# Pairing the transfers of K and x, splitting the constants, and moving two gathers, in an attention and mixture-of-experts kernel

## The chip, the core and the metric

The kernel runs on one core of one Trainium2 chip. The metric is the device time of one execution in microseconds (us); lower is better. The engines are called as in the profile: PE is TensorE (PEld its weight loads), DVE is VectorE, ACT is ScalarE, POOL is GpSimd, SP is SyncE, which only issues transfers here. A queue named after an engine (SPq, ACTq, POOLq) is the list of transfers that the engine issues, in program order.

## The reference

Attention within chunks of 64 tokens, for 8 batches of 8 heads with 576 tokens and 64 columns, then a layer of 8 experts on the 4608 rows of 512 columns that attention gives. A row goes to its best expert only where its skip score is positive.

```python
def _attn_ref(q, k, v):
    B, H, S, D = q.shape                       # 8, 8, 576, 64
    ...
    scores = scale * np.matmul(q_c, k_c.transpose(0, 1, 2, 4, 3))
    scores = scores - np.max(scores, axis=-1, keepdims=True)
    attn = np.exp(scores)
    attn = attn / (np.sum(attn, axis=-1, keepdims=True) + 1e-09)
    out = np.matmul(attn, v_c)
    return out.reshape(B, H, S, D).astype(np.float32)

def _moe_ref(x, w_skip, w_gate, w1, w2):
    do_compute = x @ w_skip > 0
    out = x.copy()
    xc = x[do_compute]
    logits = xc @ w_gate
    e_idx = np.argmax(logits, axis=1)
    ...
    for e in range(E):
        mask = e_idx == e
        h = np.maximum(xc[mask] @ w1[e], 0.0)
        y[mask] = gate_w[mask, None] * (h @ w2[e])
    out[do_compute] = xc + y
    return out.astype(np.float32)
```

## The kernel before

**Attention.** The 4608 rows are 36 tiles of 128. For each tile SP loads Q (256 KB), K (two transfers of 128 KB) and V (260 KB). K lands in a block-diagonal tile: the even partitions in half 0, the odd ones in half 1 (`load_qk`, lines 134 to 140), the rest having been set to zero once at the start (lines 149 and 155), so that one matmul against the block-diagonal K gives the scores of two heads. There are six K buffers of one tile each, six Q and six V buffers.

The loop over tiles (line 687) is software-pipelined. In iteration i PE does the scores of tile i (`pe_scores`), the weighted sum with V of tile i-2 (`pe_pv`), the transposes of x of tile i-3 (`pe_xtrans`), the router's logits of tile i-4 (`pe_logits`) and the transposes of the exponentials of tile i-1 (`pe_ptrans`). ACT copies the scores out of PSUM (`ac_scores`), takes the exponentials (`ac_exp`) and copies the two kinds of transposes (`ac_ptrans`, `ac_hi`). DVE takes the maxima (`ve_max`), normalizes into x (`ve_norm`) and makes the low halves of the split numbers (`ve_lo`). POOL subtracts the maxima (`po_sub`). The order of the instructions on each engine is the order of these calls; each engine works through its list in order.

**Transfers.** In iteration i SP issues Q and K of tile i+5 and V of tile i+4. In iterations 2 to 9 it adds one piece of w1 of the first expert (`load_piece`); ACT casts the piece three iterations later and DVE splits it (`conv_w1`). In iterations 10 to 26 it adds the store of one finished tile of x (`store_x`, line 702); the stores pause in iterations 27 to 30 and go on with three tiles each in 31 to 35, where the eight w2 pieces of the first expert follow them, two in each of the iterations 32 to 35. Each transfer is given one of eight completion counters in turn, and its issue waits until the transfer that had this counter before has landed.

**Constants.** All [128, ...] constants lie in one tensor that one transfer brings into `csb`: the identity for the transposes, the router's weights (`wsg`), the counting tables. DVE and POOL turn them into working form in iterations 1 to 7 (`more_constants`).

**Early experts.** Tokens are routed in four groups of 8, 9, 8 and 11 tiles (`route`). As soon as two groups are routed, two blocks of the first expert are known; their rows are gathered back from `out` by POOL (`early_gather`), which is allowed from iteration `GATHER_AT` + m on for block m, and three iterations later PE transposes them (`early_xt`, line 656; the transposes are line 485, ACT's cast 486, DVE's split 487). At most one such event happens in an iteration. After the loop the matmuls of the first expert's first layer (`l1_steps`, line 496) follow.

**Experts.** The other experts' weights (512 KB pieces) are loaded, cast and split while PE works through the blocks, up to the end.

Of the kernel before, what the change touches and what calls it, by code (L numbers as in the profile page):

```python
# [112 lines left out]
def moe_attention_kernel(ctx: ExitStack, tc: tile.TileContext, qk: bass.AP, vv: bass.AP, cst: bass.AP, crow: bass.AP, wall: bass.AP, out: bass.AP):  # L113
    nc = tc.nc
# [17 lines left out]
    kbd = [ap.tile([P, 2, DM], F32, name=f"k{i}", bufs=1) for i in range(KB)]  # L132

    def load_qk(t):
        if t < NT:
            T[t]["q"] = ap.tile([P, DM], F32, name="q", bufs=QB)
            nc.sync.dma_start(T[t]["q"], qk[t, 0])
            T[t]["k"] = kbd[t % KB]
            for a in range(2):
                (nc.scalar if a and t < 2 else nc.sync).dma_start(T[t]["k"].rearrange("(d h) a f -> h d a f", h=2)[a, :, a], qk[t, 1].rearrange("(d h) f -> h d f", h=2)[a])  # L140
# [153 lines left out]
    def ve_norm(t):  # L294
        o, rr = T[t].pop("o")
        nc.vector.reciprocal(rr, rr)
        x = ap.tile([P, DM], F32, name="x", bufs=XB)
# [2 lines left out]
        xq.append((t, x))  # L300

    xq = []

    def store_x(n):
        for _ in range(min(n, len(xq))):
            t, x = xq.pop(0)
            nc.sync.dma_start(out[t * P:(t + 1) * P, :], x)
# [691 lines left out]
```

## Time and profile before

| what | value |
|---|---|
| time, median of 3 runs | 346.68 us (345.04 to 348.3) |
| time of the profiled execution | 345.18 us |
| its span (first to last instruction) | 343.3 us |
| granted TensorE clock, mean | 0.994 |
| PE busy | 322.5 us (94%) |
| DVE busy | 254.3 us (74%) |
| ACT busy | 186.9 us (54%) |
| POOL busy | 110.3 us (32%) |
| moved by DMA | 81.85 MB, 238 GB/s on average |
| loads of Q, K, V, issues | 36, 72, 36 |
| stores of x, issues | 36 |

In the rows of the profile the first number of a timeline row is the start in us and the second the time that the row's instructions took; `[0.55 <-DMA k<-in_qk]` is idle time of the engine before it, and what ended it. In rows of waits stand the total in us, how often, and the longest. In rows of transfers stand their number, the KB of each and the median us from issue to landing. In rows of windows each engine's busy us comes with its number of instructions, then the granted clock, the DMA engines' busy share and the rate.

### The profile page before, as it was taken

What the parts mean: (1) busy time and instruction counts of PE and PEld (TensorE: products, weight loads), DVE (VectorE), ACT (ScalarE), POOL (GpSimd) and SP (SyncE); (2) the same over time, 40 slices, a digit from 0 to 9 for tenths busy, and PEclk for the clock granted to TensorE, in tenths of its full rate; (3) what the DMA queues carried; (4) which work ended last, traced back from release to release, by engine and by line L of the source; (5) the groups of instructions that cost most, each with busy time, mean ns of one, the idle gap of its engine ahead of it and who ended that gap; (6) DMA issues with size and microseconds to landing.
All of it is one profiled execution on the core that took longest, in us unless ns stands there. A gap on an engine that the chain in (4) does not pass through costs nothing.

```text
span 343.3 us, 10130 instructions
## 1 busy us (share of the span) xinstructions
PE 322.5 (94%) x3996; PEld 231.4 (67%) x3996; DVE 254.3 (74%) x489; ACT 186.9 (54%) x361; POOL 110.3 (32%) x110
## 2 busy tenths in 40 slices
PE   7798899999999988999899999999999999999990
PEld 4586788888888877845655456747647659587670
DVE  3668798887988877786769999966867868667230
ACT  1568787787777867403557444554454544456020
POOL 8233323334325405116700347233433322120111
PEclk9999999999999999999999999999999999999997
DMA  7999999999999998009956778767667666562001
GB/s 233 307 323 314 344 347 327 296 309 303 319 331 322 362 324 326 2 11 349 349 190 225 231 257 275 240 201 245 201 187 269 214 216 207 188 213 93 32 25 31
DMA packets 34981, 81.85 MB, mean 238 GB/s; under 512 B 4831, under 2 KB 4832, under 8 KB 34930
## 3 DMA queue, kind: packets, MB, share of 16 engines
q1 hardware_dynamic: 31378, 70.94, 62.6%
q0 software_dynamic: 3104, 9.33, 7.2%
q10 hardware_dynamic: 448, 0.89, 0.7%
q8 instruction: 33, 0.54, 0.6%
q14 instruction: 18, 0.15, 0.1%
HBM read 67.11 MB, written 14.17 MB: 237 GB/s over the span
## 4 chain that ended last, share of the span: by engine, by line
PE 51%; DVE 6%; ACT 2%; issue 1%; POOLq 0%; DVEq 0%; ACTq 0%
PE sp L521 26%; PE hp L496 20%; PE sp L528 3%; PE xt L485 2%; DVE ys L540 2%; DVE ht L501 2%; DVE wset L226 1%; ACT wset L368 1%; ACT ht L500 0%; DVE xt L487 0%; POOLq L995 0%; ACT wst L371 0%; DVE ex L398 0%; ACT wset L225 0%; DVE one L444 0%
## 5 line engine op out<-in xcount | busy, mean ns | idle before, releaser
L496 PEld LDWEIGHTS <-wset 128*128 128x128 f16 x960 | 79.2, 98 | 24.0 <-issue 7.8
L496 PE MATMUL hp<-xt,wset 128*128 128x288 f16 (+8 forms) x900 | 91.4, 262 | 3.5 <-DVE ht L501 3.5
L521 PE MATMUL sp<-wset,ht 128*128 128x512 f16 (+7 forms) x504 | 91.6, 380 | 0.0
L226 DVE SCALAR_TENSOR_TENSOR wset<-wst,wset 128x1024 f16<-128x1024 f32 x56 | 67.6, 1216 | 9.0 <-ACT wset L225 8.9
L521 PEld LDWEIGHTS <-ht 128*128 128x128 f16 (+7 forms) x504 | 40.9, 102 | 40.9 <-issue 1.9
L225 ACT ACTIVATE wset<-wst 128x1024 f16<-128x1024 f32 x56 | 57.9, 1049 | 4.1 <-DMA wst<-in_wall 4.1
L261 POOL TENSOR_TENSOR sc<-sc,mx 128x512 f32<-128x512 f32 x34 | 35.9, 1055 | 70.4 <-DVE mx L252 70.4
L500 ACT ACTIVATE ht<-hp 128x288 f16<-128x288 f32 (+8 forms) x75 | 26.9, 360 | 55.4 <-PE hp L496 54.2
L229 POOL DMA_INDIRECT out<-ys,sidx x18 | 24.9, 1386 | 99.6 <-DVE ys L540 84.8
L501 DVE SCALAR_TENSOR_TENSOR ht<-hp,ht 128x288 f16<-128x288 f32 (+8 forms) x75 | 28.4, 391 | 18.8 <-ACT ht L500 18.1
L242 PE MATMUL spq<-k,q 128*64 128x128 f32 x576 | 40.2, 283 | 0.9 <-DMA k<-in_qk 0.8
L242 PEld LDWEIGHTS spq<-k,q 128*64 128x64 f32 x576 | 31.6, 139 | 7.8 <-issue 6.6
L486 ACT ACTIVATE xt<-xt 128x512 f16<-128x512 f32 (+7 forms) x20 | 10.2, 512 | 43.8 <-PE xt L485 43.8
L252 DVE TENSOR_REDUCE mx<-sc 128x8 f32<-128x512 f32 x34 | 23.2, 683 | 10.6 <-ACT sc L247 9.8
L229 POOL DMA_INDIRECT xg<-out,sidx x18 | 25.5, 1414 | 7.5 <-issue 4.3
L298 DVE TENSOR_TENSOR x<-o,rr 128x512 f32<-128x512 f32 x36 | 24.9, 692 | 3.5
L277 ACT ACTIVATE ps<-pt 128x512 f32<-128x512 f32 x36 | 21.5, 597 | 10.3 <-PE pt L272 9.9
L247 ACT ACTIVATE sc<-spq 128x512 f32<-128x512 f32 x34 | 20.2, 595 | 12.2 <-PE spq L242 12.2
L323 DVE SCALAR_TENSOR_TENSOR xs<-xp,xs 128x512 f16<-128x512 f32 x36 | 24.5, 682 | 1.6 <-ACT xs L318 1.4
L285 PE MATMUL o<-v,ps 64*64 64x65 f32 x1152 | 25.4, 224 | 0.1
L272 PE MATMUL pt<-csb,px 128*128 128x128 f32 x144 | 23.2, 284 | 2.0 <-ACT px L265 1.9
L313 PE MATMUL xp<-csb,x 128*128 128x128 f32 x144 | 23.9, 286 | 1.2 <-issue 0.6
(129 smaller groups left out, 335.2 us busy)
## 6 DMA issues: line engine op xcount, KB each, us to landing
wst<-in_wall SPq DMA_DIRECT2D x56, 512.0 KB, 4.3
q<-in_qk SPq DMA_DIRECT2D x36, 256.0 KB, 5.0
out<-x SPq DMA_DIRECT2D x36, 256.0 KB, 5.1
v<-in_vv SPq DMA_DIRECT2D x35, 260.0 KB, 4.6
k<-in_qk SPq DMA_DIRECT2D x70, 128.0 KB, 4.6
wst<-in_wall SPq DMA_DIRECT2D x16, 256.0 KB, 4.6
csb<-in_cst ACTq DMA_DIRECT2D x1, 348.5 KB, 5.1
xg<-out,sidx POOLq DMA_INDIRECT x18, 6.4
```

The costliest lines, as they stand in the source:

```text
L225: nc.scalar.activation(w[:, 0, fc, :], st, AF.Copy, scale=SW)
L226: nc.vector.scalar_tensor_tensor(w[:, 1, fc, :], st, SW, w[:, 0, fc, :], op0=ALU.mult, op1=ALU.subtract)
L229: ins = nc.gpsimd.indirect_dma_start(**kw)
L242: nc.tensor.matmul(sp[halves[c], 2 * j:2 * j + 2, :], q[:, c, j, :], k[:, c, j], start=True, stop=True, skip_group_check=True)
L261: nc.gpsimd.tensor_tensor(T[t]["sc"], T[t]["sc"], mx, op=ALU.subtract)
L285: nc.tensor.matmul(o[halves[c], a, j * VW:(j + 1) * VW], pt[halves[a], j, halves[c]], v[halves[a], c, j, :], start=True, stop=True, skip_g ...
L298: nc.vector.tensor_tensor(x.rearrange("p (j a d) -> p a j d", j=KC, a=2), o[:, :, :, :D], rr.to_broadcast([P, 2, KC, D]), op=ALU.mult)
L323: nc.vector.scalar_tensor_tensor(xs[:, 1], T[t].pop("xp"), SX, xs[:, 0], op0=ALU.mult, op1=ALU.subtract)
L496: nc.tensor.matmul(hp, w()[:, a, fc, j * P:(j + 1) * P], xt[:, b, j, :n], start=(m == 0), stop=(m == 11))
L500: nc.scalar.activation(ht[:, 0, fc, :n], hp, AF.Relu)
L501: nc.vector.scalar_tensor_tensor(ht[:, 1, fc, :n], hp, 0.0, ht[:, 0, fc, :n], op0=ALU.max, op1=ALU.subtract)
L521: nc.tensor.matmul(y[c * P // cg:c * P // cg + n], ht[:, a, fc, o:o + n], w[:, b, fc, P * KC:], start=(f == 0 and m == 0), stop=(f == fw - ...
```

## The change

K buffers hold two tiles each, three of them. From tile 2 on, K of an even and the following odd tile are loaded together, in two transfers of 256 KB (one for each half of the partitions), in odd iterations and behind the scores of that iteration. The stores of x take two tiles at a time (512 KB): in the even iterations 10 to 26, then two pairs, one, two, one, two in the iterations 31 to 35; the last two tiles are stored singly. The identity has a transfer and a tile of its own (`idt`, 64 KB); the other constants follow V of tile 1 on SP's queue, and the casts of the router's weights and of `iota` move to iterations 3 to 5. At the start Q of tile 2 and half of K of tiles 2 and 3 are issued by ACT. `GATHER_AT` goes from 31 to 30.

```diff
-QB, KB, VB, AHEAD, VAHEAD = 6, 6, 6, 5, 4
+QB, KB, VB, AHEAD, VAHEAD = 6, 3, 6, 5, 4
...
-XB = 16
+XB = 8
...
-GATHER_AT = 31
+GATHER_AT = 30
...
-    kbd = [ap.tile([P, 2, DM], F32, name=f"k{i}", bufs=1) for i in range(KB)]
+    kbd = [ap.tile([P, 2, 2, DM], F32, name=f"k{i}", bufs=1) for i in range(KB)]
...
+    def load_k(t, n=2, eng=(nc.sync, nc.sync)):
+        if t < NT:
+            kp = kbd[t // 2 % KB]
+            u = slice(t % 2, t % 2 + n)
             for a in range(2):
+                eng[a].dma_start(kp.rearrange("(d h) t a f -> h d t a f", h=2)[a, :, u, a], qk[t:t + n, 1].rearrange("t (d h) f -> h d t f", h=2)[a])
+            for i in range(n):
+                T[t + i]["k"] = kp[:, t % 2 + i]
...
-    load_qk(0)
-    load_qk(1)
-    nc.scalar.dma_start(csb, cst)
-    load_v(0)
-    load_qk(2)
-    nc.sync.dma_start(rsb, crow)
-    load_v(1)
-    load_qk(3)
-    load_v(2)
-    load_qk(4)
-    load_v(3)
+    two = nc.sync, nc.scalar
+    for t in range(2):
+        load_q(t)
+        load_k(t, 1, two)
+    nc.scalar.dma_start(idt, cst[:, :P])
+    load_q(2, nc.scalar)
+    load_k(2, 2, two)
+    load_v(0)
+    load_q(3)
+    load_v(1)
+    nc.sync.dma_start(csb, cst[:, P:])
+    load_v(2)
+    load_q(4)
+    load_k(4)
+    load_v(3)
+    nc.sync.dma_start(rsb, crow)
...
-        x = ap.tile([P, DM], F32, name="x", bufs=XB)
+        if t % 2 == 0:
+            xpair[0] = ap.tile([P, 2, DM], F32, name="x", bufs=XB)
+        x = xpair[0][:, t % 2]
...
+        if t >= NT - 2:
+            xq.append((t, 1, x))
+        elif t % 2:
+            xq.append((t - 1, 2, xpair[0]))
...
-            nc.sync.dma_start(out[t * P:(t + 1) * P, :], x)
+            t, m, x = xq.pop(0)
+            o = out[t * P:(t + m) * P, :]
+            nc.sync.dma_start(o if m == 1 else o.rearrange("(t p) f -> p t f", t=m), x)
...
-        load_qk(i + AHEAD)
+        load_q(i + AHEAD)
         on(pe_scores, i)
+        if i % 2:
+            load_k(i + AHEAD)
...
-        store_x(0 if i < X_FROM or X_HOLD <= i < X_REST else 1 if i < X_HOLD else 3)
+        store_x(0 if i < X_FROM or X_HOLD <= i < X_REST else 1 - i % 2 if i < X_HOLD else 1 + i % 2)
```

The order on SP's queue at the start, from the first transfer on; the waits in brackets name the completion counters (DMAHW0 to DMAHW7) and the engines that cleared the K buffers. Before:

```order
L137 DMA q<-in_qk 128x512
L140 DMA k_82<-in_qk 64x512 [waits Pool_49]
L137 DMA q<-in_qk 128x512
L140 DMA k_83<-in_qk 64x512 [waits Pool_49]
L137 DMA q<-in_qk 128x512
L140 DMA k_84<-in_qk 64x512 [waits DMAHW1_49,DVE_49]
L140 DMA k_84<-in_qk 64x512 [waits DMAHW2_49]
L163 DMA rsb<-in_crow 1x360 [waits DMAHW3_49]
L145 DMA v<-in_vv 128x520 [waits DMAHW4_49]
L137 DMA q<-in_qk 128x512 [waits DMAHW5_49]
L140 DMA k_85<-in_qk 64x512 [waits DMAHW6_49,Pool_49]
L140 DMA k_85<-in_qk 64x512 [waits DMAHW7_49]
```

Now:

```order
L137 DMA q<-in_qk 128x512
L144 DMA k_82<-in_qk 64x512 [waits Pool_49]
L137 DMA q<-in_qk 128x512
L144 DMA k_82<-in_qk 64x512 [waits Pool_49]
L144 DMA k_83<-in_qk 64x2x512 [waits DMAHW1_49,DVE_49]
L151 DMA v<-in_vv 128x520 [waits DMAHW2_49]
L137 DMA q<-in_qk 128x512 [waits DMAHW3_49]
L151 DMA v<-in_vv 128x520 [waits DMAHW4_49]
L178 DMA csb<-in_cst 128x569 [waits DMAHW5_49]
L151 DMA v<-in_vv 128x520 [waits DMAHW6_49]
L137 DMA q<-in_qk 128x512 [waits DMAHW7_49]
L144 DMA k_84<-in_qk 64x2x512 [waits DMAHW0_49,Pool_49]
```

K of tile 3 stood in rows 11 and 12 and is now part of row 5; Q of tile 2 has left SP's queue, and V of tiles 0 to 2 and the constants stand between the K of the first four tiles and that of tiles 4 and 5.

The order on SP's queue for two iterations in the middle of attention (iterations with stores), before:

```order
L137 DMA q<-in_qk 128x512
L140 DMA k_82<-in_qk 64x512 x2
L145 DMA v<-in_vv 128x520
L307 DMA out<-x 128x512
L137 DMA q<-in_qk 128x512
L140 DMA k_83<-in_qk 64x512 x2
L145 DMA v<-in_vv 128x520
L307 DMA out<-x 128x512
```

Now:

```order
L137 DMA q<-in_qk 128x512
L144 DMA k_82<-in_qk 64x2x512 x2
L151 DMA v<-in_vv 128x520
L137 DMA q<-in_qk 128x512
L151 DMA v<-in_vv 128x520
L328 DMA out<-x 128x2x512
```

Ten transfers have become seven; K is issued in the odd, x in the even iteration.

The order on PE at the end of the loop, from the transposes of iteration 34 to the first matmul of the first layer (`l1_steps`), without the logits' rows (lines 330 and 351); `rk<-csb,xg` are the transposes of an early block. Before:

```order
L272 MATMUL pt<-csb,px 128x128 x4
L485 MATMUL rk<-csb,xg 128x128 x4
L242 MATMUL spq_156<-k_87,q 64x128 x8
L285 MATMUL o<-v,ps 64x65 x16
L313 MATMUL xp<-csb,x 128x128 x4
...
L272 MATMUL pt<-csb,px 128x128 x4
L485 MATMUL rk<-csb,xg 128x128 x4
L496 LDWEIGHTS wset
L496 MATMUL spq_157<-xt_176,wset 128x256
```

Now:

```order
L287 MATMUL pt<-idt,px 128x128 x4
L506 MATMUL rk<-idt,xg 128x128 x4
L257 MATMUL spq_153<-k_84,q 64x128 x8
L300 MATMUL o<-v,ps 64x65 x16
L334 MATMUL xp<-idt,x 128x128 x4
...
L287 MATMUL pt<-idt,px 128x128 x4
L517 LDWEIGHTS wset
L517 MATMUL spq_154<-xt_173,wset 128x256
```

The second block's transposes no longer stand right ahead of the first layer; they have taken the place of the first block's, which have moved one iteration up.

More of the change, by code (lines that the diff above doesn't have):

```diff
@@ L131, in moe_attention_kernel, with load_q @@
     halves = (slice(0, CH), slice(CH, P))
-    kbd = [ap.tile([P, 2, DM], F32, name=f"k{i}", bufs=1) for i in range(KB)]
-    def load_qk(t):
+    kbd = [ap.tile([P, 2, 2, DM], F32, name=f"k{i}", bufs=1) for i in range(KB)]
+    def load_q(t, eng=nc.sync):
         if t < NT:
             T[t]["q"] = ap.tile([P, DM], F32, name="q", bufs=QB)
-            nc.sync.dma_start(T[t]["q"], qk[t, 0])
-            T[t]["k"] = kbd[t % KB]
+            eng.dma_start(T[t]["q"], qk[t, 0])
+    def load_k(t, n=2, eng=(nc.sync, nc.sync)):
+        if t < NT:
+            kp = kbd[t // 2 % KB]
+            u = slice(t % 2, t % 2 + n)
             for a in range(2):
-                (nc.scalar if a and t < 2 else nc.sync).dma_start(T[t]["k"].rearrange("(d h) a f -> h d a f", h=2)[a, :, a], qk[t, 1].rearrange("(d h) f -> h d f", h=2)[a])
+                eng[a].dma_start(kp.rearrange("(d h) t a f -> h d t a f", h=2)[a, :, u, a], qk[t:t + n, 1].rearrange("t (d h) f -> h d t f", h=2)[a])
+            for i in range(n):
+                T[t + i]["k"] = kp[:, t % 2 + i]
     def load_v(t):
@@ L144, in load_v @@
             T[t]["v"] = ap.tile([P, 2, KC, VW], F32, name="v", bufs=VB)
-            (nc.sync if t else nc.scalar).dma_start(T[t]["v"], vv[t])
+            nc.sync.dma_start(T[t]["v"], vv[t])
     man = tc.manual_schedule()
     man.__enter__()
-    nc.vector.memset(kbd[0][:, 1], 0.0)
+    nc.vector.memset(kbd[0][:, 0, 1], 0.0)
     ones = cpool.tile([P, P], F16, name="ones")
@@ L153, in moe_attention_kernel @@
     nc.vector.memset(zeros, 0.0)
-    for i, k in enumerate(kbd):
-        (nc.vector if i in (2, 4) else nc.gpsimd).memset(k if i else k[:, 0], 0.0)
-    csb = cpool.tile([P, CCOLS], F32, name="csb")
-    rsb = cpool.tile([1, RCOLS], F32, name="rsb")
-    load_qk(0)
-    load_qk(1)
-    nc.scalar.dma_start(csb, cst)
-    load_v(0)
-    load_qk(2)
-    nc.sync.dma_start(rsb, crow)
-    load_v(1)
-    load_qk(3)
-    load_v(2)
-    load_qk(4)
-    load_v(3)
+    nc.gpsimd.memset(kbd[0][:, 0, 0], 0.0)
+    nc.gpsimd.memset(kbd[0][:, 1], 0.0)
+    for m in range(1, KB):
+        for i in range(2):
+            (nc.vector, nc.gpsimd)[m - 1].memset(kbd[m][:, i], 0.0)
+    idt = cpool.tile([P, P], F32, name="idt")
+    csb = cpool.tile([P, CCOLS - P], F32, name="csb")
+    rsb = cpool.tile([1, RCOLS], F32, name="rsb")
+    two = nc.sync, nc.scalar
[5 more added lines that the diff above has]
+    load_k(2, 2, two)
+    load_v(0)
+    load_q(3)
[5 more added lines that the diff above has]
+    load_v(3)
+    nc.sync.dma_start(rsb, crow)
     nc.scalar.activation(cpool.tile([P, 1], F32, name="first"), ones[:, 0:1], AF.Exp)
@@ L180, in C @@
         lo, hi = (_C if name in _C else _R)[name]
-        return (csb if name in _C else rsb)[:, lo:hi]
-    ident = C("ident")
+        return csb[:, lo - P:hi - P] if name in _C else rsb[:, lo:hi]
+    ident = idt
     upper = cpool.tile([P, P], F16, name="upper")
@@ L197, in more_constants @@
     def more_constants(i):
-        if i == DIRECT - 1:
+        if i == 3:
             w = C("wsg").rearrange("p (k n) -> p k n", k=KC)
@@ L201, in more_constants @@
             nc.vector.scalar_tensor_tensor(wsg[:, :, 1], w, SW, wsg[:, :, 0], op0=ALU.mult, op1=ALU.subtract)
-        elif i in (3, 4):
-            r = slice((i - 3) * CH, (i - 2) * CH)
+        elif i in (4, 5):
+            r = slice((i - 4) * CH, (i - 3) * CH)
             nc.vector.tensor_copy(iota[:, r], C("iota")[:, r].unsqueeze(2).to_broadcast([P, CH, G]))
@@ L296, in ve_norm @@
         nc.vector.reciprocal(rr, rr)
[L297 removed]
+        if t % 2 == 0:
+            xpair[0] = ap.tile([P, 2, DM], F32, name="x", bufs=XB)
+        x = xpair[0][:, t % 2]
         nc.vector.tensor_tensor(x.rearrange("p (j a d) -> p a j d", j=KC, a=2), o[:, :, :, :D], rr.to_broadcast([P, 2, KC, D]), op=ALU.mult)
         T[t]["x"] = x
[L300 to L302 removed]
+        if t >= NT - 2:
+            xq.append((t, 1, x))
+        elif t % 2:
+            xq.append((t - 1, 2, xpair[0]))
+    xq, xpair = [], [None]
     def store_x(n):
         for _ in range(min(n, len(xq))):
[L306 to L307 removed]
+            t, m, x = xq.pop(0)
+            o = out[t * P:(t + m) * P, :]
+            nc.sync.dma_start(o if m == 1 else o.rearrange("(t p) f -> p t f", t=m), x)
     def pe_xtrans(t):
```

## The prediction

> **What bounds the kernel now.** I read the chain of waits first, then the windows by stage, then who waited for whom in the first 136 us, then the PE rows in time.
>
> ```profile
> PE 51%; DVE 6%; ACT 2%; issue 1%; POOLq 0%; DVEq 0%; ACTq 0%
> ```
>
> ```profile
> core 0: us, PE busy (x) PEld busy (x) DVE busy (x) ACT busy (x) POOL busy (x), PEclk, DMA share, GB/s
> ...
> 24.00:40.00 16.00, 13.76 (x292) 11.34 (x293) 12.06 (x24) 12.88 (x29) 4.59 (x6) 1.00 0.96 331
> ...
> 56.00:72.00 16.00, 16.00 (x345) 13.89 (x342) 13.41 (x26) 12.49 (x29) 5.34 (x6) 1.00 0.93 291
> ```
>
> The chain is PE's, and PE is busy without a hole in 56 to 72 us at full clock. The change touches only attention and its tail; the expert blocks behind it run the same program, so the end moves by what PE gains or loses in attention. Two things matter there: the holes of PE (2.2 us of 16 in 24 to 40 us), and DMA, which is 93 to 96% busy and so may have no room for a late transfer.
>
> ```profile
> ACT wset L363 <- DMA wst<-in_wall: 2.1, 3, 1.3
> ...
> PE pt L272 <- ACT px L265: 1.9, 3, 1.3
> ```
>
> ```profile
> 10.28 0.65 PE L272 MATMUL pt<-csb,px 128*128 128x128 f32 x4 [1.31 <-ACT px L265]
> 13.72 1.09 PE L242 MATMUL spq<-k,q 128*64 128x128 f32 x16 [0.55 <-DMA k<-in_qk]
> 16.98 1.09 PE L242 MATMUL spq<-k,q 128*64 128x128 f32 x16 [0.24 <-DMA k<-in_qk]
> 26.10 0.20 PE L330 MATMUL lg<-wsg,xs 128*128 128x18 f16 x2 [0.77 <-issue]
> 26.63 0.66 PE L272 MATMUL pt<-csb,px 128*128 128x128 f32 x4 [0.34 <-ACT px L265]
> ```
>
> The reader is to see which holes a transfer opened: 0.55 us at tile 3 and 0.24 us at tile 4 wait for K itself; 0.34 us at 26.63 us waits for an exp that stood behind a weight cast on ACT. The 1.31 us at 10.28 us is the first tile's own max, subtract and exp, and stays. The 0.77 us is "issue": nothing in the trace that this change moves.
>
> **The change part by part.**
>
> *Start: K pair 2/3 ahead of V, identity alone, other constants behind V of tile 1.*
>
> ```profile
> 8.66 1.12 SPq L140 DMA_DIRECT2D k<-in_qk  x2
> ...
> 10.97 1.12 SPq L140 DMA_DIRECT2D k<-in_qk  x2
> ```
>
> From K of tile 3 at 8.66 us to K of tile 4 at 10.97 us SP issues one tile's loads without a pause: 2.31 us for 0.79 MB, so SP itself caps them at about 340 GB/s, and K of tile 3 is the one that came 0.55 us late. After, K of tiles 2 and 3 is issued in the place of K of tile 2, half of it on ACT's queue, and SP issues two transfers for what took it four (1.1 us less a pair). ACT computes nothing before the first exp, which PE has at 10.28 us, so its five issues (the last behind the landing of tile 0's Q) hold nothing up. I remove the 0.55 us. The identity alone lands sooner, but the first transposes wait for the exp anyway: 0. The other constants now go out ahead of V of tile 2; their first use on DVE stands behind the max of tile 3, whose scores start at 13.72 us before, so what hides them is some 4 us of landing time behind an issue near 9 us: 0. Without that cover DVE would stop, in iteration 3, for as long as they are late. The pair 4/5 puts 262 KB more ahead of tile 4's scores: 0.8 us at 331 GB/s, against an SP that is no longer the cap. Bounds for tile 4: its 0.24 us goes, or grows by 0.8; I leave it. **Term 1: -0.55 us (bounds -0.8 to +0.25: both waits go, or tile 3's goes and tile 4's grows by 0.8).**
>
> *Weights of the first expert.* Eight w1 pieces are issued behind the K and V of three later tiles.
>
> ```profile
> 20.41 0.43 SPq L357 DMA_DIRECT2D wst<-in_wall  x1
> ...
> 24.95 0.63 ACT L363 ACTIVATE wset<-wst 128x512 f16<-128x512 f32 x1 [1.30 <-DMA wst<-in_wall]
> ```
>
> The bytes ahead of the first piece are the same before and after (tiles 0 to 7 of Q and K, 0 to 6 of V, the constants: 6.4 MB). It lands at 24.95 us, ACT wanted it 1.30 us before. The stretch from 9 to 25 us need only run 8% faster to cover that. PE's own loss is 1.9 - 1.31 = 0.6 us behind exp; ACT's is 2.1 us. A part of ACT's delay runs on into later tiles, a part hides under the 0.77 us hole: I take 0.8, near the PE row. **Term 2: -0.8 us (bounds -2.1 to 0).**
>
> *K and stores in pairs, from tile 10 on.* Bytes are equal; SP issues 7 transfers for two tiles instead of 10. Each transfer names one of eight completion counters in turn and waits for the one eight before it, so eight are in flight: 8 x 206 KB on average before, 8 x 294 KB after.
>
> ```profile
> DMA packets 9434, 16.90 MB, mean 313 GB/s; under 512 B 1287, under 2 KB 1287, under 8 KB 9422
> ...
> k<-in_qk SPq DMA_DIRECT2D x34, 128.0 KB, 4.6
> ```
>
> ```profile
> DMA packets 4611, 8.78 MB, mean 351 GB/s; under 512 B 545, under 2 KB 545, under 8 KB 4607
> ...
> out<-x SPq DMA_DIRECT2D x19, 256.0 KB, 5.4
> ```
>
> The first fence is 56 to 110 us (mixed sizes), the second 111 to 136 us, where every transfer is 256 KB: with 24% more in flight the rate is 12% higher and the landing 0.8 us longer. That is the nearest row to a queue of pairs, so I take 351 GB/s: 1.053 MB a tile in 3.00 us against 3.36 us at 313. It is needed, since the cover of K shrinks:
>
> ```profile
> 47.15 1.16 SPq L140 DMA_DIRECT2D k<-in_qk  x2
> ...
> 88.53 1.13 SPq L140 DMA_DIRECT2D k<-in_qk  x2
> ```
>
> ```profile
> 57.28 1.09 PE L242 MATMUL spq<-k,q 128*64 128x128 f32 x16
> ...
> 94.42 1.09 PE L242 MATMUL spq<-k,q 128*64 128x128 f32 x16
> ```
>
> These are K of tiles 16 and 28 and their scores. The second half is issued some 0.55 us after the row's start and lands 4.6 us later: 52.3 us for 57.28, a cover of 5.0 us; 93.7 us for 94.42, a cover of 0.7 us. PE takes (94.42 - 57.28) / 12 = 3.10 us a tile and DMA is slower, until stores pause at iteration 27. After, an even tile's K has 262 KB of its neighbour's K and 262 KB of one more stored tile ahead of it: 1.5 us at 351 GB/s. PE being 1.35 us earlier (terms 1 and 2) takes cover too. Against these 2.85 us stands 3.36 - 3.00 = 0.36 us a tile, 4.3 us over the 12 tiles: a cover of 0.7 + 4.3 - 2.85 = 2.2 us is left. **Term 3: 0 (bounds 0 to +1.0, worked out under the rivals).** The Trainium skill, "DMA: Bandwidth & Descriptors", section "Bandwidth", gives 341 GB/s for a transfer of 1 MB; by an estimate from it a tile would take 3.09 us, the gain over 12 tiles would be 3.2 us and the cover 1.1 us instead of 2.2: the sum stays, the wall of the first rival comes nearer. The 351 GB/s of this trace, eight smaller transfers at once, is above it, and the trace decides.
>
> *Early gathers a tile sooner.* Order changes in one spot on PE, ACT and DVE: the second early block's transposes, its cast and its split move from iteration 35 to 34 (the first block's from 34 to 33).
>
> ```profile
> 119.92 0.60 PE L485 MATMUL rk<-csb,xg 128*128 128x128 f32 x4
> 121.32 1.32 PE L496 MATMUL spq<-xt,wset 128*128 128x256 f16 x8 [0.80 <-ACT xt L486]
> ```
>
> Now the first layer's matmuls come right behind the transposes that feed them and stop 0.80 us for the cast. After, logits and transposes of iteration 35 lie between; the work only moves, so its own 0.60 us costs nothing. The matmuls' second half, which needs DVE's split, may gain 0.3 us more; I leave that out. For it the gathers must land in time:
>
> ```profile
> 103.57 1.04 POOL L261 TENSOR_TENSOR sc<-sc,mx 128x512 f32<-128x512 f32 x1 [2.43 <-DVE mx L252]
> 106.52 1.04 POOL L261 TENSOR_TENSOR sc<-sc,mx 128x512 f32<-128x512 f32 x1 [1.91 <-DVE mx L252]
> 107.75 1.21 POOL L229 DMA_INDIRECT xg<-out,idx  x1 [0.19 <-DMA v<-in_vv]
> ```
>
> The first gather goes from behind the subtraction of 106.52 us to behind that of 103.57 us, so POOL reaches it at 104.6 us. It waits for the store of tiles 16 and 17, now one transfer, and the next subtraction is queued behind it on POOL, with that tile's exp and PE's transposes of it behind. Between 104.61 and 106.52 us POOL has 1.9 us of idle for the wait and 1.2 us of issue; 0.7 us of waiting are covered, each us beyond would reach the exp. **Term 4: -0.8 us (bounds -1.1 to 0).**
>
> *Tail.* Three stores in each of the iterations 31 to 35 become two pairs, one, two, one, two, so one or two more tiles stand ahead of a w2 piece.
>
> ```profile
> 116.78 1.03 SPq L357 DMA_DIRECT2D wst<-in_wall  x2
> ```
>
> ```profile
> 124.90 0.62 ACT L368 ACTIVATE wset<-wst 128x512 f16<-128x512 f32 x1
> ```
>
> ```profile
> wst<-in_wall SPq DMA_DIRECT2D x4, 256.0 KB, 7.2
> ```
>
> The first w2 piece is issued at 116.78 us, lands 7.2 us later (median of 116 to 124 us), at 124.0, and is cast at 124.90: 0.9 us of cover. It now has one more tile ahead (0.75 us at 351 GB/s) and ACT comes 2.15 us earlier, so it is 2.0 us short unless DMA is that much earlier too; by term 3's rate DMA gains 4.3 us by then, which hides it. Without that, the two relus behind the cast on ACT, and PE's next matmuls behind them, would be late. **Term 5: 0 (0 to +1).**
>
> **Sum.** -0.55 - 0.8 + 0 - 0.8 + 0 = -2.15 us. The profiled execution took 345.18 us (span 343.3 and 1.9 around it), so it would take 343.0. It lies 1.5 us under the median of 346.68; the four executions shown (346.68, 345.04, 348.3, 345.18) average 346.3, and I put the forecast there: 346.3 - 2.15 = 344.1 us, 0.6% faster. A measurement of this kernel tells about 1% (3.5 us) from no change: under 342.8 is faster, over 349.8 slower.
>
> **The rivals.**
>
> *DMA is the wall, so the early gain is lost.* If pairs move no more than 313 GB/s, K of tile 28 lands at 93.7 + 0.524 MB / 313 GB/s = 95.4 us, 1.0 us behind the 94.42 us of before, whatever was won earlier; terms 1 and 2 are gone, term 3 is +1.0, term 4 stays: +0.2 us, 346.5. For it: DMA share of 93 to 96%, and the whole attention stage at this share. Against it: 351 GB/s with 256 KB transfers.
>
> *Pairs run slower than singles.* A pair holds one of the eight counters until its slowest part is there, so if the parts are uneven fewer are in flight in effect, and PE is fed at the DMA's pace from tile 16 until the stores pause. It decides from 313 GB/s downwards: at 300 (the 56 to 72 us row has 291) a tile takes 3.51 us, 0.15 more, 18 tiles from the first store at iteration 10: +2.7, so 346.5 + 2.7 = 349.2 us, slower than before. Against it: 256 KB stores land in 5.4 us and K's 128 KB in 4.6, so a doubled transfer pays far less than double.
>
> *PE's "issue" holes shrink too.*
>
> ```profile
> 33.38 0.27 PE L330 MATMUL lg<-wsg,xs 128*128 128x18 f16 x5 [0.49 <-issue]
> 40.68 0.35 PE L330 MATMUL lg<-wsg,xs 128*128 128x18 f16 x8 [0.99 <-issue]
> ```
>
> They come 7.3 us apart (26.10, 33.38, 40.68) in a stage with DMA at 96%, 2.25 us together, and not in 56 to 72 us. If they are waits on crowded DMA and the new order thins it, the time is 344.1 - 2.2 = 341.9 us. Against it: DMA will stay as full.
>
> **How the numbers follow.** Forecast 0.56, the wall 0.19, slower pairs 0.11, holes shrink 0.14. The range starts between the third rival and the forecast with its terms at their lower bounds (-0.8 - 2.1 - 1.1 = -4.0, 342.3), lowered to 341.4 for the scatter of the runs, and reaches over the wall into the slower pairs, to 347.3. Faster by over 1% needs 342.8: most of the third rival and a seventh of the forecast, 0.20. Slower needs 349.8: the far end of slower pairs, 0.05. Between: 0.75.
>
> **What would show it.** Right: no DMA wait at PE's scores of tile 3; the waits of ACT on wst under 0.8 us in total; no wait on ACT xt before the first layer's matmuls of line 496; DMA at 340 GB/s or more from 56 to 110 us and K's cover at tile 28 above 1 us. The end of attention then comes some 2 us earlier and nothing after 152 us has another length. Wrong: PE waiting for DMA K at even tiles 24 to 32 (the wall), POOL's first gather waiting over 0.7 us with holes at PE's transposes after it, or ACT waiting for w2 pieces at 122 us.

## The result and the profile after

The changed kernel takes 342.45 us (median of 6 runs, 341.25 to 343.93) against 346.35 us before (median of 6, 345.04 to 348.3): 3.9 us less, ratio 0.989 with a 95% interval from 0.9849 to 0.9931. Measured again with other runs (experiment e9) it is 343.23 against 346.40 us, ratio 0.9903 (0.987 to 0.9936). The forecast was 344.1 us, so the effect is some 1.5 to 1.8 times the 2.15 us of the sum. The profiled execution took 341.25 us, its span is 339.5 us.

First the chain of waits of the changed kernel, from its page:

```profile
PE 78%; DVE 6%; DMA 5%; ACT 4%; issue 3%; SPq 2%; POOLq 0%; DVEq 0%; ACTq 0%
```

These shares cannot be set beside the 51% of before: that chain could be followed back only to 128.6 us, this one to the first microsecond. What it holds of DMA are K loads in the first 16 us and one w1 piece, here with its start and length in us:

```profile
26.82 6.29 DMA wst<-in_wall
```

So a wait for w1 still lies on the path. The windows of the same two stages as before, with the columns named in the prediction:

```profile
24.00:40.00 16.00, 15.22 (x328) 12.79 (x320) 13.75 (x26) 14.20 (x32) 5.63 (x7) 1.00 1.03 362
56.00:72.00 16.00, 16.00 (x342) 13.78 (x340) 13.51 (x30) 12.49 (x29) 5.28 (x6) 1.00 1.05 394
```

PE is busy 15.22 us of 16 where it was 13.76; DMA moves 362 and 394 GB/s where it moved 331 and 291. Then PE's rows in time, the scores of tiles 3 (12.79 us), 4 (16.21 us) and 35 (114.86 us), the transposes with a hole from 24 to 44 us, the largest hole behind them, and the first layer's first matmuls (117.72 us):

```profile
12.79 1.09 PE L257 MATMUL spq<-k,q 128*64 128x128 f32 x16
...
16.21 1.09 PE L257 MATMUL spq<-k,q 128*64 128x128 f32 x16 [0.39 <-DMA k<-in_qk]
...
25.12 0.66 PE L287 MATMUL pt<-idt,px 128*128 128x128 f32 x4 [0.24 <-ACT px L280]
28.45 0.66 PE L287 MATMUL pt<-idt,px 128*128 128x128 f32 x4 [0.25 <-ACT px L280]
34.82 0.66 PE L287 MATMUL pt<-idt,px 128*128 128x128 f32 x4 [0.29 <-ACT px L280]
...
109.49 0.34 PE L300 MATMUL o<-v,ps 64*64 64x65 f32 x6 [0.84 <-issue]
...
114.86 1.09 PE L257 MATMUL spq<-k,q 128*64 128x128 f32 x16
...
117.72 1.04 PE L517 MATMUL spq<-xt,wset 128*128 128x256 f16 x8
```

Tile 3 has no wait for K any more, while that of tile 4 is 0.39 us where it was 0.24; the 0.80 us wait for xt is gone (117.72 for 121.32 us); the three issue holes of 24 to 44 us are gone, and a new one of 0.84 us stands at 109.49 us. What ACT and PE waited for in the first 136 us:

```profile
PE pt L287 <- ACT px L280: 2.0, 4, 1.2
PE o L300 <- issue: 1.0, 2, 0.8
...
ACT wset L384 <- DMA wst<-in_wall: 1.0, 3, 0.3
```

ACT waits 1.0 us for w1 pieces instead of 2.1 us. DMA of the changed kernel from 56 to 110 us:

```profile
DMA packets 9647, 18.28 MB, mean 338 GB/s; under 512 B 948, under 2 KB 948, under 8 KB 9635
...
k<-in_qk SPq DMA_DIRECT2D x14, 256.0 KB, 4.9
```

The same view from 12 to 44 us, the stage of the w1 pieces:

```profile
DMA packets 6545, 12.07 MB, mean 377 GB/s; under 512 B 728, under 2 KB 729, under 8 KB 6537
...
q<-in_qk SPq DMA_DIRECT2D x12, 256.0 KB, 5.4
k<-in_qk SPq DMA_DIRECT2D x12, 256.0 KB, 5.8
```

And that stage in the kernel before:

```profile
DMA packets 5824, 10.42 MB, mean 326 GB/s; under 512 B 794, under 2 KB 794, under 8 KB 5817
...
q<-in_qk SPq DMA_DIRECT2D x11, 256.0 KB, 5.1
k<-in_qk SPq DMA_DIRECT2D x21, 128.0 KB, 5.0
```

The rate rises from 326 to 377 GB/s, and a landing takes 0.3 to 0.8 us longer. The 338 GB/s of 56 to 110 us is a mean over a stage in which DMA first moves 394 GB/s (56 to 72 us) and then 288 (88 to 110 us), where SP mostly waits for PE to free buffers. SP's row of K of tiles 28 and 29 shows it:

```profile
76.59 1.27 SPq L144 DMA_DIRECT2D k<-in_qk  x2
```

PE's first row of the scores of tile 28:

```profile
91.40 0.87 PE L257 MATMUL spq<-k,q 128*64 128x128 f32 x11
```

The second half is issued some 0.6 us behind the row's start and lands 4.9 us later: 82.1 us for a use at 91.40, a cover of 9.3 us where it was 0.7.

### The profile page after: what moved, and what is told of

It reads as the page before. It is cut to its first block, busy times and chain, and to the rows that moved or that the text cites. A ratio compares the mean times of both kernels' runs of the same rounds, so it can differ in the third digit from the quotient of the medians.

```text
span 339.5 us, 10061 instructions
## 1 busy us (share of the span) xinstructions
PE 320.9 (95%) x3996; PEld 230.9 (68%) x3996; DVE 255.0 (75%) x489; ACT 187.3 (55%) x361; POOL 109.8 (32%) x110
## 4 chain that ended last, share of the span: by engine, by line
PE 78%; DVE 6%; DMA 5%; ACT 4%; issue 3%; SPq 2%; POOLq 0%; DVEq 0%; ACTq 0%
PE sp L542 26%; PE hp L517 20%; PE spq L257 8%; PE o L300 5%; PE xp L334 5%; PE pt L287 4%; PE sp L549 3%; DMA k<-in_qk 3%; PE xt L506 2%; DMA wst<-in_wall 2%; DVE ys L561 2%; PE lg L351 2%; DVE ht L522 2%; DVE wset L241 1%; ACT wset L389 1%
## 5 line engine op out<-in xcount | busy, mean ns | idle before, releaser
L257 PE MATMUL spq<-k,q 128*64 128x128 f32 x576 | 39.3, 279 | 0.8 <-DMA k<-in_qk 0.8
L257 PEld LDWEIGHTS spq<-k,q 128*64 128x64 f32 x576 | 30.8, 137 | 7.5 <-issue 6.2
L300 PEld LDWEIGHTS o<-v,ps 64*64 64x64 f32 x1152 | 20.4, 133 | 7.8 <-issue 6.7
L287 PE MATMUL pt<-idt,px 128*128 128x128 f32 x144 | 23.3, 284 | 2.5 <-ACT px L280 2.0
```

Of the source, the lines that this page charges most:

```text
L257: nc.tensor.matmul(sp[halves[c], 2 * j:2 * j + 2, :], q[:, c, j, :], k[:, c, j], start=True, stop=True, skip_group_check=True)
L287: nc.tensor.transpose(pt[:, j, :], px[:, j * P:(j + 1) * P], ident)
L300: nc.tensor.matmul(o[halves[c], a, j * VW:(j + 1) * VW], pt[halves[a], j, halves[c]], v[halves[a], c, j, :], start=True, stop=True, skip_g ...
```

## The experiments

Each was timed beside the kernel before on the same chip; ratios are to that kernel, with 95% intervals. On the chip of e1 to e8 the granted clock was 0.92 to 0.95 from 136 to 200 us in every kernel traced there, and the kernel before takes 2 to 3% longer than on the chip of e9 to e12; only ratios, and the stages ahead of 120 us, are compared with the others. Even there the clock was not full everywhere: from 12 to 44 us it is 0.95 in e1, e3, e5 and e7 and 0.88 in e6, so PE is slower there and may ask less of DMA. The changed kernel itself was not run on that chip.

### e1: the early gathers alone

Edit of the kernel before:

```diff
-GATHER_AT = 31
+GATHER_AT = 30
```

> The kernel before with one edit: early gathers, and the transposes and casts behind them, a tile sooner. Theory (each part adds up): the 0.80 us wait for ACT's xt cast ahead of the first layer's matmuls goes and nothing takes its place, so 345.5 us against 346.35 (-0.8), and PE's rows up to 100 us stand where they stood. Rival (the wait only moves): in the changed kernel PE is 3.7 us ahead at tile 32, only 2.2 us at tile 35 and 3.6 us again behind xt, so what the sooner gather gives at xt it took between tiles 32 and 35; then 346.3 us, with a new hole of 0.5 to 1 us near 110 to 114 us.

Measured: 352.85 against 353.73 us, ratio 0.9992 (0.9961 to 1.0022), -0.3 us with bounds from -1.4 to +0.8: this cannot tell -0.8 from nothing. The trace can. PE's scores of tiles 32 and 35 and the first layer's first matmuls in e1:

```profile
107.37 1.09 PE L242 MATMUL spq<-k,q 128*64 128x128 f32 x16
...
117.78 1.09 PE L242 MATMUL spq<-k,q 128*64 128x128 f32 x16
...
120.64 1.04 PE L496 MATMUL spq<-xt,wset 128*128 128x256 f16 x8
```

The same three rows of the kernel before:

```profile
107.76 1.09 PE L242 MATMUL spq<-k,q 128*64 128x128 f32 x16
...
117.06 1.09 PE L242 MATMUL spq<-k,q 128*64 128x128 f32 x16
...
121.32 1.32 PE L496 MATMUL spq<-xt,wset 128*128 128x256 f16 x8 [0.80 <-ACT xt L486]
```

From tile 32 to the first layer it is 13.27 us, of which 0.36 us is an issue hole at 112.30 us, so 12.91; before 13.56. From tile 35 alone it looks like 1.4 us (2.86 for 4.26), but the transposes that moved ahead cost their 0.6 us there. So -0.65 us in this pair, and the rival's new hole is at least not bound to the gathers: e3, with sooner gathers and no hole in that stretch, takes 12.68 us.

### e2: K tile by tile, all else as changed

Edit of the changed kernel:

```diff
-    load_k(4)
+    load_k(4, 1)
...
-        if i % 2:
-            load_k(i + AHEAD)
+        load_k(i + AHEAD, 1)
```

> The changed kernel, but K of tile 4 and later goes tile by tile in two transfers of 128 KB, as before; start, stores in pairs and early gathers stay as changed. Theory (K in pairs): the 2.5 us that PE wins from tile 6 to tile 13 come from K's pairs, because SP issues less and the DMA queues stay full; without them the issue holes of PE near 26, 33 and 40 us are back (2.2 us together) and ACT waits for w1 pieces: 342.45 + 2.5 = 345.0 us. Rival (the start): the order of the first loads sets how far DMA is ahead when the w1 pieces come; then 342.5 us and no holes.

Measured: 351.97 us, ratio 0.9924 (0.9887 to 0.996). What PE and ACT waited for up to 136 us:

```profile
PE pt L287 <- ACT px L280: 6.5, 6, 2.9
ACT wset L384 <- DMA wst<-in_wall: 5.7, 5, 3.0
```

And its window of 12 to 44 us, the last number being GB/s:

```profile
12.00:44.00 32.00, 27.05 (x568) 22.48 (x566) 23.73 (x46) 22.99 (x50) 10.82 (x14) 1.00 0.92 306
```

The rate falls to 306 GB/s, below the 326 of before, ACT waits 5.7 us for w1 and PE 6.5 us behind exp: the theory's mechanism, and worse than before. The ratio, though, lies between the two theories, and its profiled execution took 354.3 us, 2.3 us above the median of its runs, so its waits are larger than usual. What start, paired stores and gathers bring without K's pairs (0.4 to 1.1%) is not shown by this trace.

### e3: the first loads as before, all else as changed

Edit of the changed kernel:

```diff
-    nc.scalar.dma_start(idt, cst[:, :P])
-    load_q(2, nc.scalar)
-    load_k(2, 2, two)
-    load_v(0)
-    load_q(3)
-    load_v(1)
-    nc.sync.dma_start(csb, cst[:, P:])
+    nc.scalar.dma_start(csb, cst)
+    load_v(0)
+    load_q(2)
+    load_k(2, 1)
+    nc.sync.dma_start(rsb, crow)
+    load_v(1)
+    load_q(3)
+    load_k(3, 1)
     load_v(2)
...
```

> The changed kernel with the first loads as before: K of tiles 2 and 3 one by one behind V of tile 0 and 1, all constants in one transfer ahead of V of tile 0; from tile 4 on K in pairs, stores in pairs, early gathers as changed. Theory (K in pairs): only the wait of 0.55 us for K of tile 3 is back, 342.45 + 0.5 = 343.0 us, and there is no issue hole from 24 to 44 us. Rival (the start): 342.45 + 3 = 345.5 us, with the holes near 26, 33 and 40 us back.

Measured: 348.81 us, ratio 0.9873 (0.9814 to 0.9933). The rate from 12 to 44 us is 367 GB/s, and of its waits up to 136 us these two:

```profile
PE pt L286 <- ACT px L279: 1.7, 2, 1.0
...
ACT wset L383 <- DMA wst<-in_wall: 0.7, 1, 0.7
```

No issue hole falls between 24 and 44 us. The start is not what makes DMA early: the rival falls. PE waits 1.10 us for K of tile 2 instead.

### e4: single stores, all else as changed

Edit of the changed kernel:

```diff
-XB = 8
+XB = 16
...
-        store_x(0 if i < X_FROM or X_HOLD <= i < X_REST else 1 - i % 2 if i < X_HOLD else 1 + i % 2)
+        store_x(0 if i < X_FROM or X_HOLD <= i < X_REST else 1 if i < X_HOLD else 3)
```

> The changed kernel, but x is stored tile by tile with the old rule (one a tile from 10 to 26, three from 31 on). Theory (K in pairs): PE is no different up to tile 10, the rate from 56 to 110 us falls towards the 313 GB/s of before, K's cover at tile 28 shrinks from 10 us to between 2 and 8 us, and no wait comes of it: 342.5 us. Rival (all transfers in pairs are needed): SP falls behind again and K is waited for near tile 28, 343.5 us or more.

Measured: 349.01 us, ratio 0.9877 (0.9817 to 0.9937). The time is as the theory had it, the rate is not: from 56 to 88 us it is

```profile
DMA packets 6254, 11.51 MB, mean 360 GB/s; under 512 B 695, under 2 KB 695, under 8 KB 6247
```

against 303 GB/s before and 373 in the changed kernel. Paired stores add 13 GB/s that nobody needs.

### e5 and e6: the same number of bytes in more transfers

Edit of the changed kernel in e5, each K pair as four transfers:

```diff
             for a in range(2):
-                eng[a].dma_start(kp.rearrange("(d h) t a f -> h d t a f", h=2)[a, :, u, a], qk[t:t + n, 1].rearrange("t (d h) f -> h d t f", h=2)[a])
+                for i in range(n):
+                    eng[a].dma_start(kp.rearrange("(d h) t a f -> h d t a f", h=2)[a, :, t % 2 + i, a], qk[t + i, 1].rearrange("(d h) f -> h d f", h=2)[a])
```

Edit of the changed kernel in e6, Q of tile 4 and later in two halves:

```diff
-            eng.dma_start(T[t]["q"], qk[t, 0])
+            for h in range(2 if t > 3 else 1):
+                r = slice(h * CH, P if t < 4 else (h + 1) * CH)
+                eng.dma_start(T[t]["q"][r], qk[t, 0, r])
```

> The changed kernel with its order and its lookahead, but each K pair as four transfers of 128 KB instead of two of 256 KB: 4.5 transfers a tile instead of 3.5, the same bytes at the same places in the queue. Theory (size of a transfer): with K tile by tile the rate from 56 to 88 us was 321 GB/s, with K in pairs 360 to 373 whatever the start and the stores; so it falls to 310 to 330 GB/s here, ACT waits for w1 pieces again (2 us or more) and PE loses 1.5 to 3 us from 24 to 50 us, ratio to before 0.992 to 0.998. Rival (order: an even tile's K is asked for earlier): the rate stays at 370 and the ratio is that of the change, 0.989.

> The changed kernel, K in pairs, but Q of tile 4 and later as two transfers of 128 KB: 4.5 transfers a tile, as with K tile by tile. Theory (size of a transfer, whichever tensor): as with quarters of K, 310 to 330 GB/s from 56 to 88 us, ratio 0.992 to 0.998. Rival (K itself: its 64 rows into every second column block are slow to write one tile at a time): 370 GB/s and 0.989.

Measured: e5 357.1 us, ratio 1.0067 (1.0034 to 1.0101); e6 362.31 us, ratio 1.02 (1.0143 to 1.0258). Both are slower than the kernel before. The window of 12 to 44 us in e5:

```profile
12.00:44.00 32.00, 27.77 (x564) 23.09 (x563) 23.14 (x44) 22.47 (x48) 10.81 (x14) 0.95 0.93 309
```

In e6:

```profile
12.00:44.00 32.00, 25.07 (x456) 21.01 (x456) 20.07 (x39) 19.31 (x41) 9.76 (x13) 0.88 1.00 278
```

(The granted clock, last column but two, cannot explain e5: e7 and e3 have 0.95 there too, with 360 and 367 GB/s. In e6 it may take part.) From 56 to 88 us, the stretch that the expectations name, the rates are 314 and 308 GB/s, as the theory had it; the ratios are worse than it had them. So neither the order nor the lookahead of the pairs helps, nor anything about K: Q in halves does the same and more. The DMA engines' busy share is 1.00 in e6 at 278 GB/s, and 0.93 in e5 at 309: the engines need longer for the same bytes, which the number of transfers does not explain, and the cause stays open. SP's rows show another part of the "more", in e6:

```profile
29.76 1.11 SPq L139 DMA_DIRECT2D q<-in_qk  x2
```

and before, one tile of loads and one w1 piece:

```profile
25.09 1.12 SPq L140 DMA_DIRECT2D k<-in_qk  x2
26.30 0.53 SPq L145 DMA_DIRECT2D v<-in_vv  x1
26.87 0.43 SPq L357 DMA_DIRECT2D wst<-in_wall  x1
27.35 0.43 SPq L137 DMA_DIRECT2D q<-in_qk  x1
27.82 1.12 SPq L140 DMA_DIRECT2D k<-in_qk  x2
```

Two halves of 64 rows take SP 1.1 to 1.3 us, one transfer of 128 rows 0.43. In the kernel before SP needs 27.82 - 25.09 = 2.73 us for 1.05 MB without a pause, which is 385 GB/s at the very best: little is left to win back what SP loses in a wait.

### e7: K in pairs alone

Edit of the kernel before:

```diff
-    kbd = [ap.tile([P, 2, DM], F32, name=f"k{i}", bufs=1) for i in range(KB)]
+    kbd = [ap.tile([P, 2, 2, DM], F32, name=f"k{i}", bufs=1) for i in range(KB)]
...
+        if i % 2:
+            load_k(i + AHEAD)
```

> The kernel before with one edit: K of tile 4 and later in pairs; first loads, single stores and early gathers as before. Theory (K in pairs carries most of the gain): 360 to 380 GB/s from 56 to 88 us, no wait of 1 us for w1 pieces or behind exp from 24 to 50 us, ratio 0.992 to 0.994 (2.2 to 2.6 us of the 3.9). Rival (the parts need one another): under 1 us, ratio 0.997 or more.

Measured: 350.31 us, ratio 0.9844 (0.9802 to 0.9885), better than either theory said, and by the intervals no worse than the whole change. 360 GB/s from 12 to 44 us, 364 from 56 to 88, and of its waits up to 136 us these two:

```profile
PE pt L286 <- ACT px L279: 1.8, 2, 1.3
...
ACT wset L378 <- DMA wst<-in_wall: 0.6, 1, 0.6
```

### e8 and e12: Q in pairs as well

Edit of the changed kernel in e8; in e12 the same, with Q of tiles 4 and 5 still single:

```diff
-            T[t]["q"] = ap.tile([P, DM], F32, name="q", bufs=QB)
-            eng.dma_start(T[t]["q"], qk[t, 0])
+            if t % 2 == 0:
+                qp[0] = ap.tile([P, 2, DM], F32, name="q", bufs=QB // 2)
...
+                eng.dma_start(qp[0], qk[t:t + 2, 0].rearrange("t p f -> p t f"))
```

> The changed kernel with Q of tile 4 and later in pairs as well (one transfer of 512 KB for two tiles): 3 transfers a tile instead of 3.5. Theory (size of a transfer): the rate is 390 GB/s or a little more, but K already lands 10 us ahead of its use, so only the rest of the waits from 16 to 46 us (1.5 us) can go, and Q of tile 4 with 256 KB more ahead of K may add 0.4 us at tile 4: ratio 0.987 to 0.990. Rival (too few transfers leave queues uneven): the rate falls under 370 GB/s and the ratio rises to 0.992.

> The changed kernel with Q in pairs as well, but only from tile 6 on: Q of tiles 4 and 5 goes singly, so that K of tiles 4 and 5 is not behind both. With pairs from tile 4 on, PE waited 2.4 us for K of tile 4, and ACT waited for no w1 piece. Theory: the wait at tile 4 falls to 0.4 us as in the changed kernel, the waits from 24 to 46 us stay small, and it beats the changed kernel of this call by 0.2 to 0.5%: ratio to before 0.984 to 0.987. Rival (nothing is left to win): the ratio of the changed kernel within 0.2%.

Measured: e8 351.03 us, ratio 0.9874 (0.982 to 0.9928); e12 344.11 us, ratio 0.9919 (0.9877 to 0.9961), with the changed kernel at 0.9903 beside it. The rate is the highest of all, 386 and 388 GB/s from 12 to 44 us, and it wins nothing: the rival holds for e12. In e8 PE waits 2.4 us for K of tile 4. The profile of e12 shows what was lost there instead:

```profile
26.32 0.18 PE L359 MATMUL lg<-wsg,xs 128*128 128x18 f16 x1 [1.34 <-issue]
...
39.82 0.31 PE L359 MATMUL lg<-wsg,xs 128*128 128x18 f16 x6 [1.26 <-issue]
```

Issue holes of 1.3 us with DMA at its best.

### e9: the changed kernel again

Nothing is edited.

> The changed kernel unaltered, as the measure for the other kernels of this call. From 12 to 44 us SP spent 24.7 us on 47 issues in it, against 27.4 us on 51 before; ratio to before 0.989 again, 377 GB/s from 12 to 44 us. If the clock that is granted behind 136 us (0.92 to 0.95 in the experiments so far, 1.00 in the first two profiles) takes part of the gain, 0.986 to 0.992.

Measured: 343.23 us against 346.40, ratio 0.9903 (0.987 to 0.9936), with 373 GB/s. Its profiled execution has these PE rows:

```profile
26.51 0.18 PE L351 MATMUL lg<-wsg,xs 128*128 128x18 f16 x1 [1.06 <-issue]
...
111.67 0.34 PE L300 MATMUL o<-v,ps 64*64 64x65 f32 x6 [1.93 <-issue]
```

3.0 us of issue holes from 8 to 117 us, where the first profile of the same kernel has 1.2. The holes come and go between executions.

What they wait for can be read from the DMA records of the traces. Among them are transfers of 16 KB on a queue named for instructions; here that queue in the kernel before, from 12 to 44 us (number, MB, share of the engines' time):

```profile
q8 instruction: 4, 0.07, 0.8%
```

In the kernel before such transfers start at 23.71, 31.01, 38.19 and 44.21 us, and its holes end at 26.10, 33.38, 40.68 and 46.62 us, 2.4 to 2.5 us later each. In e9 they start at 24.31 and 109.32 us, 2.2 and 2.4 us ahead of the ends of its two holes. Of the 45 issue holes of all fourteen traces from 8 to 117 us, 43 end 2.2 to 2.8 us behind the start of such a transfer, whether DMA moves 306 or 388 GB/s; such transfers start some 6 us apart, so chance would put few ends there. So these holes are most likely PE waiting for its own next instructions. Most of these transfers open no hole, and why some do is not shown.

### e10: one tiny transfer more a tile

Edit of the changed kernel:

```diff
         load_v(i + VAHEAD)
+        if i < 27:
+            nc.sync.dma_start(ap.tile([1, 64], F32, name="tiny", bufs=8), crow[:, :64])
```

> The changed kernel with one more transfer on SP in each of the iterations 0 to 26: 256 bytes of a constant into a tile that nobody reads, behind V. The bytes and the sizes of all other transfers stay. Theory (SP's issues are the limit): each costs SP some 0.34 us (the row of rsb), so 24.7 us of issues from 12 to 44 us become 28.5 or more of 32, as before the change; the rate falls from 377 to 320 to 350 GB/s and the ratio rises to 0.993 to 0.998. Rival A (bytes in flight under eight counters): a tiny transfer takes a counter as well, 4.5 transfers a tile as with K tile by tile or in quarters: about 306 GB/s, ratio 1.00 or more, and SP waits for DMA. Rival B (a 128 KB transfer is slow by itself): nothing changes, 377 GB/s and 0.989.

Measured: 346.57 us, ratio 0.9969 (0.9924 to 1.0013); the changed kernel beside it 0.9903. The window of 12 to 44 us:

```profile
12.00:44.00 32.00, 27.61 (x580) 23.16 (x572) 24.59 (x47) 23.97 (x53) 10.92 (x15) 1.00 0.98 335
```

What PE and ACT waited for up to 136 us:

```profile
PE pt L287 <- ACT px L280: 4.1, 4, 1.8
...
ACT wset L384 <- DMA wst<-in_wall: 3.2, 4, 1.8
```

One of the tiny transfers on SP:

```profile
24.42 0.29 SPq L723 DMA_DIRECT2D tiny<-in_crow  x1
```

256 bytes in 0.29 us of SP's time bring back the late w1 pieces. The theory had the time and the rate right, but not what SP does: its rows from 12 to 44 us add up to 21.6 us for 50 transfers, not to 28.5, and it waits. What it waits for is landings (waits of SP in the same stretch, the largest two): 

```profile
SPq L137 <- DMA q<-in_qk: 1.8, 2, 1.4
SPq L144 <- DMA v<-in_vv: 1.5, 2, 1.1
```

All waits of SP for landings add up to 8.1 us there, against 5.2 us in the changed kernel. That is rival A's mechanism: a tiny transfer takes one of the eight counters. Rival A's rate of 306 was too low a figure; rival B (size by itself) falls.

### e11: w1 pieces and single stores on POOL's queue

Edit of the kernel before:

```diff
-        nc.sync.dma_start(st, wall[FIRST, f, :, r])
+        (nc.sync if kind else nc.gpsimd).dma_start(st, wall[FIRST, f, :, r])
...
-            nc.sync.dma_start(out[t * P:(t + 1) * P, :], x)
+            (nc.gpsimd if n == 1 else nc.sync).dma_start(out[t * P:(t + 1) * P, :], x)
```

> The kernel before with the eight w1 pieces and the single stores of iterations 10 to 26 issued by POOL instead of SP; sizes, bytes and K tile by tile as before. SP issues 4 transfers a tile instead of 5. Theory (SP's issues or its counters are the limit): the rate from 12 to 44 us rises from 326 to 350 to 375 GB/s, ACT waits less than 1 us for w1 pieces, ratio 0.993 to 0.997. Rival (size: 128 KB transfers are slow by themselves): 326 GB/s stays, ratio 1.00 or above, because POOL's issues delay its subtractions.

Measured: 345.96 us, ratio 0.9978 (0.9943 to 1.0014). The rate from 12 to 44 us is 340 GB/s and the ratio just outside the theory's range, both a little short of it; from 56 to 88 us, with the stores on POOL and K still in 128 KB, the rate is:

```profile
DMA packets 5816, 11.58 MB, mean 362 GB/s; under 512 B 878, under 2 KB 878, under 8 KB 5808
```

against 303 before. ACT waits for no w1 piece and PE never behind exp (tile 0's wait is hidden by one of 1.03 us for K). It is not the 128 KB of a transfer that is slow. The time gains little: PE loses 3.3 us in issue holes in this execution, and keeps the 0.80 us before the first layer.

### All of them side by side

Transfers a tile are those on SP's queue in the iterations that bring w1 pieces; what is in flight is at most eight of them, of 1.05 MB a tile; PE's waits are from 8 to 117 us.

| kernel | transfers a tile | in flight, MB | GB/s, 12 to 44 us | ACT waits for w1, us | PE behind exp, us | PE issue holes, us | ratio |
|---|---|---|---|---|---|---|---|
| before | 5 | 1.68 | 326 | 2.1 | 1.9 | 2.9 | 1 |
| e1 | 5 | 1.68 | 327 | 2.8 | 3.9 | 0.4 | 0.9992 |
| e2 | 5 | 1.68 | 306 | 5.7 | 6.5 | 2.6 | 0.9924 |
| e5 | 5 | 1.68 | 309 | 3.6 | 4.0 | 4.5 | 1.0067 |
| e6 | 5 | 1.68 | 278 | 5.6 | 4.9 | 2.2 | 1.02 |
| e10 | 5 | 1.68 | 335 | 3.2 | 4.1 | 1.9 | 0.9969 |
| e11 | 4 and 1 on POOL | 1.83 | 340 | 0 | 0 | 3.3 | 0.9978 |
| after | 4 | 2.1 | 377 | 1.0 | 2.0 | 1.2 | 0.989 |
| e9 | 4 | 2.1 | 373 | 0.8 | 1.5 | 3.0 | 0.9903 |
| e3 | 4 | 2.1 | 367 | 0.7 | 1.7 | 0.2 | 0.9873 |
| e4 | 4 | 2.1 | 374 | 1.3 | 2.0 | 0.3 | 0.9877 |
| e7 | 4 | 2.1 | 360 | 0.6 | 1.8 | 1.2 | 0.9844 |
| e8 | 3.5 | 2.4 | 386 | 0.3 | 1.5 | 0.4 | 0.9874 |
| e12 | 3.5 | 2.4 | 388 | 1.1 | 1.3 | 5.5 | 0.9919 |

The rate follows the number of transfers on SP's queue, whichever tensor they carry; e6 alone falls further than its number says. Bytes in flight over the time to landing give the size of it: 1.68 MB / 5.0 us = 336 GB/s for 326 before, 2.1 MB / 5.5 us = 382 for 377 after. That the eight are nearly always in use can be estimated from the rows of transfers: numbers times times to landing, over 32 us, give 7.9 in flight before, 8.0 and 7.3 in the changed kernel and e9, and 7.6 in e12. PE's wait behind exp is 4.2 us on average over the six kernels with 5 transfers on SP's queue, and 1.7 us over the seven with 4 or 3.5 (some 1.2 us of it is tile 0's and stays). The kernels with the full clock from 12 to 44 us alone give the same two means: 4.2 us (before, e2, e10) and 1.7 us (after, e4, e8, e9, e12).

## Why the prediction was right, and where its sizes were not

**The rate (term 3).** The mechanism that the prediction named, eight counters and so more bytes in flight with larger transfers, is the one that e10 and e11 bear out; in the kernel before SP's own time, 27.4 us of rows in 32, is close behind it: with 7.9 of the eight in flight the counters bind there most of the time, but which of the two binds moment by moment is not separated. The size was off: 351 GB/s was taken from 111 to 136 us, while the changed kernel does 377 from 12 to 44 and 373 from 56 to 88 us. The cover of K at tile 28 came out at 9.3 us where 2.2 were worked out. The term itself, 0, is right, since PE gets nothing from a cover that grows; the step failed in what it did not do, to take the higher rate back to 12 to 44 us, where transfers were late.

**First expert's weights (term 2).** This is the likeliest term to be mis-sized: -0.8 us was taken from PE's 0.57 us behind exp in one execution. K in pairs alone (e7), which should have given this term and nothing else, gave 5.0 us by the medians, and 4.1 to 7.0 us by the interval of its ratio. In the traces the wait behind exp shrinks by 2.5 us if all kernels with 5 transfers are taken (4.2 against 1.7), and by 1.1 us if only before and e1 are, the two that run the old program up to there (2.9 against 1.8 of the five with 4). The profile of before was the mildest of its kind: e1, the same program up to iteration 30, has 3.9 us where it has 1.9. The bound of -2.1 was nearer.

**Start (term 1).** No wait for K at tile 3: right. PE starts the scores of tile 5 at 19.38 us instead of 19.92, -0.54 for -0.55. That the two numbers agree is luck: PE's first transposes start 0.31 us sooner in that execution (9.97 for 10.28 us), and tile 4's wait grew by 0.15 us, inside its bounds. It is no sure gain either: in e9 the same kernel starts them at 19.99 us, with 0.86 us and 0.54 us of waiting for K of tiles 2 and 4, and e3, without the new start, has the same ratio as the changed kernel.

**Early gathers (term 4).** -0.8 forecast, -0.65 to -0.9 by the traces (13.56 us from tile 32 to the first layer before, 12.91 in e1, 12.68 in e3, 12.89 after without its hole of 0.84 us). The time of e1 alone cannot confirm it. The first gather waited 0.19 us on POOL, inside its cover.

**Tail (term 5).** 0, right: the first w2 piece is issued at 104.9 us instead of 116.8 and landed 9 us ahead of its cast.

**The sum.** With -1.1 to -2.5 us for term 2 it becomes -2.45 to -3.85 us, against a measured -3.9 and -3.2 us: that term accounts for a sixth to all of what was missing, and with its size known from so few executions it cannot be closed further. The profiled executions speak for the sum as it stood: without their issue holes their spans are 340.4 us before and 338.3 and 338.7 us (e9) changed, 1.7 to 2.1 us less. But the profile of before lies 1.2 us under that kernel's median, and what its usual execution has more of is in no trace. That the two profiled executions differ by 3.9 us is partly luck: in that pair PE's wait behind exp is the same (1.9 and 2.0 us), and the issue holes give 1.7 us (2.9 to 1.2) which e9 does not have. Nor do the parts add up by experiment: e7 alone gave no less than the whole, and all without K's pairs (e2) gave 0.4 to 1.1%.

**The rivals.** The wall and the slower pairs did not come: DMA's rate rose. The busy share of 93 to 96% on which the wall rested was no ceiling: it is 1.03 from 24 to 40 us and 1.05 from 56 to 72 us in the changed kernel. The prediction's first reading, that the chain is PE's, says nothing of attention, since that chain goes back only to 128.6 us. The holes rival gave 341.9 us, near the measured time, and the first profile seemed to prove it. It is not shown: with few transfers the holes range from 0.2 to 5.5 us, with many from 0.4 to 4.5, and the kernel with the highest rate has the largest sum. They end 2.2 to 2.8 us behind the start of an instruction transfer (e9), and the traces do not tie them to a crowded DMA.

Of the signs that were to show it, two were missed narrowly: ACT waits 1.0 us for w1 pieces, where under 0.8 was named, and the rate from 56 to 110 us is 338, where 340 was named, because SP ran out of free buffers (from 76 to 110 us it waits 14.3 us for PE's weighted sums, after which V's buffers are free).
